# Two raw products side by side on smaller first loads, and later scales between partitions by DMA transposes

## The chip, the cores and the metric

The kernel runs on one core of a Trainium2 chip. The core has engines that each work through their own program in order: PE (TensorE, matrix products; PEld is its loading of the stationary operand), DVE (VectorE), ACT (ScalarE), POOL (GpSimd) and SP (SyncE), which here issues nearly all DMA transfers. Engines wait for each other through semaphores. The metric is the device time of one execution in microseconds (us); the median of several runs is compared. Differences under about 0.2% can't be told from run to run.

## What is computed

Two independent halves are joined along the last axis. A is attention with 32 heads of 32 and a sliding window of 256 over 2048 positions, between two projections; B is a Fourier mixing, two products with cosine and sine matrices on each side of x. All tensors are float32.

```python
def _A_ref(x, wqkv, wo):
    B, S, D = x.shape                # 1, 2048, 1024
    H = 32; Dh = D // H; W = 256
    qkv = (x @ wqkv).reshape(B, S, 3, H, Dh).transpose(2, 0, 3, 1, 4)
    q, k, v = qkv[0], qkv[1], qkv[2]
    scores = einsum("bhqd,bhkd->bhqk", q, k) * (Dh ** -0.5)
    scores = where(causal and within W, scores, -1e9)
    o = einsum("bhqk,bhkd->bhqd", softmax(scores), v)
    return o.transpose(0, 2, 1, 3).reshape(B, S, D) @ wo

def _B_ref(x, dft_seq_re, dft_seq_im, dft_hid_re, dft_hid_im):
    a = einsum("bsd,ed->bse", x, dft_hid_re)
    b = einsum("bsd,ed->bse", x, dft_hid_im)
    return einsum("ts,bse->bte", dft_seq_re, a) - einsum("ts,bse->bte", dft_seq_im, b)

return concatenate([A, B], axis=-1)
```

## The kernel before

**Split numbers and their scales.** A product of two float32 matrices is made from float16 parts: each operand is scaled by a power of two and split into a high and a low half (`split`, L124: ACT writes the high half, DVE the low one), and three products hi·hi, hi·lo, lo·hi are summed in PSUM. So every operand needs a scale before it can be split. `top` and `mean` (L142, L150) leave one number for each of the 128 partitions; `spread` (L157) reduces it to one column; and `scale_of` (L166) makes one number of the 128: PE transposes the column, broadcast over 128 columns, against the identity matrix `ident` into a PSUM tile `pt_...`, DVE reduces that to a maximum (`tensor_reduce`), cuts it to a power of two, and takes the reciprocal. In the head (`head[0]` true) the transposes sit in PE's order at a place written out by hand (L171); later (L174) they take a bank of the three that the products rotate through, and in the last stage the bank `pv` of the attention.

**Stages.** The head does the first four q products (`pq0_0` to `pq3_0`, four groups of weights `wq` against the first quarter of x) directly on the raw float32 data, eight matmuls each (`d_mm`, L736); the scale is applied only to their result (`d_out`, L890). A dozen-odd matmuls on zeros (`warm`) run first. A loop over `order` (L930) then makes all other q, k and v products in float16, 24 matmuls each, and from its step 22 on a generator, `attention`, weaves the attention's matmuls between them (`tick`, at a rate from a table). Small jobs are attached to steps by `at(n, ...)` (L398): a weight is loaded six steps before its first use, its `w_top` runs four before, `w_finish` (scale and split) three before. The last stage runs units of seven products each (`seven`), in which the jobs are attached to positions ("turns") by `do(n, turn, ...)`: for a unit's cosine or sine matrix `u`, `u_load` three units ahead, `u_top` two ahead at turns 0 and 2, `u_scale` at turn 6, and the splits `u_step` one unit ahead, at its turns 0 to 4.

**What sets the order.** A scheduler places instructions on each engine, with hand-set constraints: PE's matmuls follow one another as written (`mm`, L112, through `fixed`); DVE's in the head do too (`vec`, through `latest`). DMA issues on SP run in order, those of the attention behind one another (`line`): `t<-hl` transposes the softmax weights of a block (128x1024 float16), `raw_u` loads the next matrix. `behind` holds the latest DVE instruction of an attention block or product, and other DVE work is placed behind it.

**Memory.** `xin` (the split x) fills the tile `reg1`; `spare` is its tail. The pool `pa` holds the products' outgoing tiles, `yq`/`yk` and `yv`, two of each.

Of the kernel before, what the change touches and what calls it, by code (L numbers as in the profile page):

```python
# [12 lines left out]
BF16 = mybir.dt.bfloat16  # L13
U8 = mybir.dt.uint8
U32 = mybir.dt.uint32
AF = mybir.ActivationFunctionType
# [3 lines left out]
P = 128  # L20
S = 2048
D = 1024
H = 32
# [30 lines left out]
def fused_kernel(ctx: ExitStack, tc: tile.TileContext, xa, wqk, wv, wo, xb, wd, cs, out):  # L54
# [25 lines left out]

    ident = const.tile([P, P], F32, name="ident")
    make_identity(nc, ident)


# [11 lines left out]

    nbank, units_on = [0], []

# [35 lines left out]

    tops, head = {}, [True]


# [19 lines left out]
    def spread(key, n):  # L157
        t = tops.pop(key)
        if n > 1:
            t1 = small.tile([P, 1], F32, tag="top0", name=f"top1_{key}")  # L160
            vec(nc.vector.tensor_reduce, t1, t, axis=AX.X, op=ALU.max)
        else:
            t1 = t
        tops[key] = t1

    def scale_of(key, v, s, down=2.0 ** -14):  # L166

        if head[0]:
            pt = ps_s.tile([P, CH], F32, tag="s", name=f"pt_{key}")[:, :P]
            with tc.issue_after(fixed[0].ins) if fixed else nullcontext():  # L170
                fixed[:] = [nc.tensor.transpose(pt, tops.pop(key).to_broadcast([P, P]), ident)]  # L171
        else:
            pt = (ps_v.tile([P, CH], F32, tag="pv", name=f"pt_{key}") if units_on else bank(f"pt_{key}"))[:, :P]
            nc.tensor.transpose(pt, tops.pop(key).to_broadcast([P, P]), ident)  # L174
# [266 lines left out]
    def x_load(c, pool=None):  # L441
        for i in range(4):
            if c == 0 or c == 2 and i < 2:
                xraw[c, i] = praw(2 * c + i).rearrange("p (d t) -> p d t", t=CH)
                nc.sync.dma_start(xraw[c, i], xa[c, i])
# [105 lines left out]
    for (kd, g), n in use.items():  # L551
        if kd in "qk" and n >= 4:
            at(n - 6, w_load, kd, g)
            at(n - 4, w_top, kd, g)
            at(n - 3, w_finish, kd, g)
    for g in range(NG):
# [6 lines left out]
    at(7, strict.__setitem__, 0, False)  # L563
    at(7, head.__setitem__, 0, False)
    at(4, x_top, 2, (0, 1))
    at(5, x_top, 2, (2, 3))
# [7 lines left out]
    at(14, wv_top, 0)  # L574
    at(15, wv_scale, 0)
    for i, n in enumerate((15, 16, 16, 17)):
        at(n, wv_split, 0, (i,))
    at(15, wv_load, 1)
    at(18, wv_top, 1)
    at(19, wv_scale, 1)  # L580
    for i, n in enumerate((19, 20, 21, 21)):
        at(n, wv_split, 1, (i,))
# [136 lines left out]

    for i in range(WARM // 3):  # L720
        nc.tensor.matmul(wps, warm[:, :P], warm, start=True, stop=True)
    w_load("q", 0, first)
    x_load(0, first)
    for g in (1, 2, 3):
        w_load("q", g, first)
    x_load(1, first)
    x_load(2)
# [8 lines left out]
    def d_mm(g, ds):  # L736
# [3 lines left out]
        for d in ds:  # L740
            mm(direct[g], wraw["q", g][:, d], xraw[0, d // 2][:, d % 2], start=(d == 0), stop=(d == ND - 1))

# [136 lines left out]

    with tc.tile_pool(name="pa", bufs=2) as pa:  # L880
        def qk_out(kd, g, c, ps, f):
            y = pa.tile([P, 2, CH], F16, tag="yq", name=f"y{kd}{g}_{c}")
            behind_act[:] = [nc.scalar.activation(y[:, 0], ps, AF.Copy, scale=f)]
# [8 lines left out]

        w_top("q", 0)
        x_top(0, (0, 1, 2, 3))
        d_mm(0, range(0, 4))
        w_scale("q", 0)
        d_mm(0, range(4, 8))
        w_top("q", 1)
        d_mm(1, range(0, 1))
        x_scale(0)  # L900
        d_known(0)
        d_mm(1, range(1, 3))
        w_scale("q", 1)
        d_known(1)
        d_out(0)
        w_split("q", 0)
        w_top("q", 2)
        d_mm(1, range(3, 8))
        x_top(1, (0, 1))
        d_out(1)  # L910
        d_mm(2, range(0, 2))
        w_scale("q", 2)
        d_known(2)
        x_top(1, (2, 3))
        d_mm(2, range(2, 8))
        w_top("q", 3)
        d_mm(3, range(0, 2))
        x_scale(1)
        x_split(1, (0, 1))
        d_out(2)  # L920
        d_mm(3, range(2, 4))
        w_scale("q", 3)
        d_known(3)
        x_split(1, (2,))
        d_mm(3, range(4, 8))
        x_split(1, (3,))
        w_split("q", 1)
        d_out(3)

        for n, (kd, g, c) in enumerate(order):  # L930
# [154 lines left out]

    units_on.append(True)
# [159 lines left out]
```

## Time and profile before

| | |
|---|---|
| median of 3 runs | 1708.01 us (1707.69 to 1711.28) |
| profiled execution, its own time | 1705.92 us |
| its span (first to last instruction) | 1703.9 us |
| mean granted TensorE clock | 1.000 |
| share of the span busy: PE / DVE / ACT / POOL | 99% / 76% / 69% / 34% |
| mean busy share of the 16 DMA engines, 200 to 400 us | 1.02 |

A row of a timeline reads: start in us, length in us, engine, line, operation, what it writes <- what it reads, shapes, count, and in brackets how long the engine had been idle and what ended that. Rows of matmuls that follow one another are merged (x10); the length of a merged row goes to the end of its last matmul, which overlaps the next row's start. Names are the program's: `wx` is where the first quarter of x lands, `raw_wq` a raw weight, `reg` any of the large tiles `reg1` and `reg2`. A float32 matmul of 512 columns appears as two instructions, so eight `d_mm` steps are sixteen.

### The profile page before, as it was taken

How to read it: one execution, taken by the hardware profiler on the slowest of the kernel's cores; microseconds unless marked ns; L12 is line 12 of the kernel's file. 1: busy time of each engine (PE TensorE's matmuls, PEld its weight loads, DVE VectorE, ACT ScalarE, POOL GpSimd, SP SyncE). 2: the span in 40 equal slices, each digit the busy share in tenths (PEclk: the TensorE clock that was granted, in tenths of full speed). 3: DMA queues.
4: the chain of work that ended last, by engine and by line, in shares of the span. 5: the costliest groups of instructions: out<-in, count | busy, mean ns of one | idle time of the engine just before them, and what ended most of it. 6: DMA issues, size and time to landing. Idle time of an engine off the chain costs nothing.

```text
span 1703.9 us, 30860 instructions
## 1 busy us (share of the span) xinstructions
PE 1693.1 (99%) x10999; PEld 851.4 (50%) x10999; DVE 1301.6 (76%) x2225; ACT 1169.3 (69%) x2035; POOL 573.8 (34%) x874
## 2 busy tenths in 40 slices
PE   9999999999999999999999999999999999999999
PEld 4444555555555554555555555555555555444444
DVE  6847788887988688887678886688886698688442
ACT  4466666676877687888678886678877687563322
POOL 0000322334444341444423474433555425411000
PEclk9999999999999999999999999999999999999999
DMA  9747999999998995887998999986999976876431
GB/s 351 244 138 241 258 289 273 289 254 305 249 231 218 207 231 122 197 203 178 226 249 246 198 183 175 232 201 120 194 167 203 228 183 136 173 184 119 116 99 75
DMA packets 469898, 348.62 MB, mean 205 GB/s; under 512 B 376944, under 2 KB 409968, under 8 KB 468848
## 3 DMA queue, kind: packets, MB, share of 16 engines
q1 hardware_dynamic: 462064, 321.48, 75.3%
q0 software_dynamic: 7680, 25.17, 9.2%
q8 instruction: 86, 1.41, 0.4%
q14 instruction: 68, 0.56, 0.1%
HBM read 166.99 MB, written 106.17 MB: 160 GB/s over the span
## 4 chain that ended last, share of the span: by engine, by line
PE 80%; DVE 7%; ACT 4%; DMA 4%; issue 3%; POOL 2%; SPq 0%; DVEq 0%; POOLq 0%; ACTq 0%
PE p_a L114 22%; PE pv L114 13%; PE p_b L114 10%; PE pk L114 9%; PE pq L114 8%; PE p_c L114 5%; PE po_a L114 5%; PE s L114 3%; PE po_b L114 2%; PE far L114 1%; PE po_c L114 1%; DMA t<-hl 1%; DMA ots<-ot 1%; DVE reg L835 1%; DVE hl L270 1%
## 5 line engine op out<-in xcount | busy, mean ns | idle before, releaser
L266 ACT ACTIVATE s<-s,bias,escs 128x256 f32<-128x256 f32 (+1 forms) x512 | 270.0, 528 | 11.7
L284 POOL TENSOR_SCALAR_AFFINE_SELECT z<-t 128x512 f16<-128x512 f16 x224 | 187.0, 841 | 159.6 <-PE pv L114 142.3
L259 ACT ACTIVATE bias<-mx,pshift,escs 128x2 f32<-128x2 f32 x256 | 98.3, 384 | 171.6 <-DVE mx L256 171.3
L270 DVE TENSOR_TENSOR hl<-s,hl 128x512 f16<-128x512 f32 (+1 forms) x256 | 170.1, 665 | 56.0 <-ACT hl L269 55.2
L114 PEld LDWEIGHTS <-reg 128*128 128x128 f16 x1344 | 128.9, 97 | 141.7
L286 POOL TENSOR_SCALAR_AFFINE_SELECT t<-t 128x512 f16<-128x512 f16 x224 | 183.8, 829 | 11.4
L114 PE MATMUL p_a<-reg,un_c 128*128 128x512 f16 x768 | 181.2, 379 | 0.4 <-ACT p_c L1068 0.2
L263 POOL TENSOR_SCALAR mark<-bias 128x1 f32<-128x1 f32 x128 | 53.1, 415 | 363.0 <-ACT bias L259 356.5
L114 PE MATMUL pk<-reg,wu_k 128*128 128x512 f16 x768 | 174.4, 379 | 0.0
L256 DVE TENSOR_REDUCE mx<-s 128x2 f32<-128x512 f32 (+1 forms) x256 | 170.9, 668 | 3.4
L114 PE MATMUL pv<-reg,reg 128*128 128x512 f16 x768 | 172.7, 379 | 0.0
L114 PEld LDWEIGHTS <-un_c 128*128 128x128 f16 x1152 | 109.9, 97 | 121.3 <-issue 2.0
L114 PEld LDWEIGHTS <-un_b 128*128 128x128 f16 x1152 | 110.0, 97 | 117.8 <-issue 1.1
L114 PEld LDWEIGHTS <-un_a 128*128 128x128 f16 x1152 | 109.7, 97 | 116.3
L269 ACT ACTIVATE hl<-s 128x512 f16<-128x512 f32 (+1 forms) x256 | 148.8, 581 | 6.4 <-DMA t<-hl 1.0
L114 PE MATMUL pq<-reg,wu_q 128*128 128x512 f16 x672 | 151.3, 379 | 0.8 <-DVE reg L121 0.5
L114 PE MATMUL p_a<-reg,un_b 128*128 128x512 f16 x576 | 136.4, 379 | 0.4 <-DVE y L1036 0.3
L114 PE MATMUL p_b<-reg,un_b 128*128 128x512 f16 x576 | 136.4, 379 | 0.3 <-DVE reg L835 0.3
L114 PE MATMUL p_a<-reg,un_a 128*128 128x512 f16 x576 | 136.6, 379 | 0.0
L114 PE MATMUL p_c<-reg,un_a 128*128 128x512 f16 x576 | 136.5, 379 | 0.0
L254 DVE COPY_PREDICATED s<-upper,far 128x256 f32<-128x256 uint32 x224 | 94.3, 421 | 46.2 <-PE s L114 44.9
L114 PEld LDWEIGHTS <-qk 96*128 96x128 f16 x1056 | 87.9, 97 | 64.3 <-issue 1.8
(208 smaller groups left out, 3153.2 us busy)
## 6 DMA issues: line engine op xcount, KB each, us to landing
raw_u<-in_cs_dram SPq DMA_DIRECT2D x64, 512.0 KB, 4.9
qk<-qk SPq DMA_DIRECT2D x64, 384.0 KB, 4.9
out_dram<-y POOLq DMA_DIRECT2D x72, 256.0 KB, 6.1
raw_wd<-in_wd_dram SPq DMA_DIRECT2D x24, 512.0 KB, 5.2
vs<-yv SPq DMA_DIRECT2D x32, 264.0 KB, 4.4
vt<-vs SPq DMA_DIRECT2D x64, 132.0 KB, 4.5
raw_wo<-in_wo_dram SPq DMA_DIRECT2D x16, 512.0 KB, 8.1
qk<-yq SPq DMA_DIRECT2D x32, 256.0 KB, 3.4
```

The source lines that it names most:

```text
L114: fixed[:] = [nc.tensor.matmul(*args, **kwargs)]
L254: nc.vector.copy_predicated(s[:, :, P:], upper2, d["far"] if nb == 3 else never2)
L256: nc.vector.tensor_reduce(mx, sv, axis=AX.X, op=ALU.max, negate=True)
L259: nc.scalar.activation(bias, mx, AF.Identity, bias=pshift, scale=es)
L263: marks[:] = [nc.gpsimd.tensor_scalar(mark, bias[:, 0:1], 1.0, None, op0=ALU.mult)]
L266: nc.scalar.activation(sv[:, h], sv[:, h], AF.Exp, bias=bias[:, h:h + 1], scale=es)
L269: nc.scalar.activation(hi, sv, AF.Copy)
L270: behind[:] = [nc.vector.tensor_tensor(lo, sv, hi, op=ALU.subtract)]
L284: nc.gpsimd.affine_select(out=z, in_=pk, compare_op=ALU.is_gt, fill=0.0, base=0, pattern=[[0, 4], [-1, P]], channel_multiplier=1)
L286: nc.gpsimd.affine_select(out=pk, in_=pk, compare_op=ALU.is_ge, fill=0.0, base=0, pattern=[[0, 4], [1, P]], channel_multiplier=-1)
L835: nc.vector.tensor_tensor(lo, src, hi, op=ALU.subtract)
```

## The change

The diff has three parts: the head (nine smaller loads, the first two raw products interleaved, other jobs reordered), the scales after the head (from step 11 of the loop on, by DMA transposes on SP instead of PE), and buffers (one tag `y` with three tiles; `ident` placed in `spare`).

```diff
-    ident = const.tile([P, P], F32, name="ident")
+    ident = spare[:, :2 * P].bitcast(F32)
     make_identity(nc, ident)
...
     tops, head = {}, [True]
+    crossing, crossed = [None], {}
...
         tops[key] = t1
+        if crossing[0]:
+            pb = crossing[0].tile([P, P], F16, tag="pb", name=f"pb_{key}")
+            nc.vector.tensor_scalar(pb.bitcast(U16), t1.bitcast(U16)[:, 1:2].to_broadcast([P, P]), 0x7F80, None,
+                                    op0=ALU.bitwise_and)
+            pc = crossing[0].tile([P, 1, P], F16, tag="pc", name=f"pc_{key}")
+            with tc.issue_after(line[0].ins) if line else nullcontext():
+                nc.sync.dma_start_transpose(pc, pb)
+            crossed[key] = pc.rearrange("p a t -> p (a t)").bitcast(BF16)
 
     def scale_of(key, v, s, down=2.0 ** -14):
 
+        if key in crossed:
+            with tc.issue_after(behind[0].ins):
+                nc.vector.tensor_reduce(v, crossed.pop(key), axis=AX.X, op=ALU.max)
+            nc.vector.tensor_scalar(v, v, 2.0 ** -100, down, op0=ALU.max, op1=ALU.mult)
+            nc.vector.reciprocal(s, v)
+            return
...
-            at(n - 3, w_finish, kd, g)
+            at(n - 3 if n < 16 else n - 2, w_finish, kd, g)
...
+    at(11, lambda: crossing.__setitem__(0, pa))
...
-    at(15, wv_scale, 0)
-    for i, n in enumerate((15, 16, 16, 17)):
+    at(16, wv_scale, 0)
+    for i, n in enumerate((16, 17, 17, 18)):
...
-    for i in range(WARM // 3):
+    for i in range(WARM // 4):
         nc.tensor.matmul(wps, warm[:, :P], warm, start=True, stop=True)
-    w_load("q", 0, first)
-    x_load(0, first)
-    for g in (1, 2, 3):
+    for g in (0, 1):
+        wraw["q", g] = first.tile([P, ND, P], F32, tag="raw", name=f"raw_wq{g}")
...
+    def w_part(g, a, b):
+        nc.sync.dma_start(wraw["q", g][:, a:b], wqk[0, g][:, a:b])
+
+    def x_part(a, b):
+        nc.sync.dma_start(xraw[0, a // 2][:, a % 2:a % 2 + b - a], xa[0, a // 2][:, a % 2:a % 2 + b - a])
+
+    for f, args in ((w_part, (0, 0, 2)), (x_part, (0, 1)), (w_part, (1, 0, 2)), (x_part, (1, 2)), (w_part, (0, 2, 8)),
+                    (x_part, (2, 4)), (w_part, (1, 2, 8)), (x_part, (4, 6)), (x_part, (6, 8))):
+        f(*args)
...
-    with tc.tile_pool(name="pa", bufs=2) as pa:
+    with tc.tile_pool(name="pa", bufs=3) as pa:
         def qk_out(kd, g, c, ps, f):
-            y = pa.tile([P, 2, CH], F16, tag="yq", name=f"y{kd}{g}_{c}")
+            y = pa.tile([P, 2, CH], F16, tag="y", name=f"y{kd}{g}_{c}")
...
-        w_top("q", 0)
-        x_top(0, (0, 1, 2, 3))
-        d_mm(0, range(0, 4))
+        for g in range(3):
+            w_top("q", g)
+        x_top(0, (0, 1))
+        d_mm(0, (0,))
+        d_mm(1, (0,))
+        d_mm(0, (1,))
+        d_mm(1, (1,))
+        d_mm(0, (2, 3))
         w_scale("q", 0)
...
-                y = pa.tile([P, H // 2, VW], F16, tag="yv", name=f"yv{g}_{t}")
+                y = pa.tile([P, H // 2, VW], F16, tag="y", name=f"yv{g}_{t}")
...
     with tc.tile_pool(name="pb", bufs=1) as pb:
+        crossing[0] = pb
```

**PE in the head.** The names are `pq_0` for a raw product (its number tells which), `wx` for x, and `pt_` for a transpose of a scale. Before, PE's rows behind the warm-up were these:

```order
L114 MATMUL pq_0_171<-wx,raw_wq_132 128x512 x4
L171 MATMUL pt_wq_176<-ident,top_wq_162 128x128
L114 MATMUL pq_0_171<-wx,raw_wq_132 128x512 x4
L114 MATMUL pq_0_188<-wx,raw_wq_138 128x512
L171 MATMUL pt_x_190<-ident,top_x_169 128x128
L114 MATMUL pq_0_188<-wx,raw_wq_138 128x512 x2
L171 MATMUL pt_wq_200<-ident,top_wq_186 128x128
L114 MATMUL pq_0_188<-wx,raw_wq_138 128x512 x5
```

After the change the same engine has, from the end of the warm-up to the end of the first two products:

```order
L116 MATMUL pq_0_171<-wx,raw_wq_129 128x512
L116 MATMUL pq_0_173<-wx,raw_wq_130 128x512
L116 MATMUL pq_0_171<-wx,raw_wq_129 128x512
L116 MATMUL pq_0_173<-wx,raw_wq_130 128x512
L116 MATMUL pq_0_171<-wx,raw_wq_129 128x512 x2
L188 MATMUL pt_wq_179<-reg_83,top_wq_162 128x128
L116 MATMUL pq_0_173<-wx,raw_wq_130 128x512 x2
L188 MATMUL pt_wq_188<-reg_83,top_wq_164 128x128
L116 MATMUL pq_0_171<-wx,raw_wq_129 128x512 x2
L116 MATMUL pq_0_173<-wx,raw_wq_130 128x512 x2
L188 MATMUL pt_x_201<-reg_83,top_x_195 128x128
L116 MATMUL pq_0_171<-wx,raw_wq_129 128x512 x2
```

The two products take turns, so that PE uses each piece of x twice before it needs the next, and the transpose of x's scale has moved from the ninth matmul to behind the twelfth. The number of raw matmuls and of the head's transposes is the same; two matmuls of the warm-up are gone.

**A scale in the last stage, on PE.** Before, around the scale of the unit's matrix that DVE reads at about 920 us (`pt_u` the transpose, `p_16` the unit's product):

```order
L114 LDWEIGHTS reg_83
L114 MATMUL p_16_b<-reg_83 128x512
L174 MATMUL pt_u_11514<-ident,top_u_11391 128x128
L114 LDWEIGHTS un_b
L114 MATMUL p_16_a<-reg_83,un_b 128x512
```

After, the row of `pt_u` is gone here and at 56 other places; no other row of PE's order behind the head has moved.

**The same scale on SP and DVE, after.** SP's rows there are these (`pb` is the column written out over 128 columns, `pc` its transpose, `t<-hl` that of a block's softmax weights):

```order
L784 DMA raw_u_0_11518<-in_cs_dram 128x1024
L289 DMA_TRANSPOSE t_11420<-hl_11417 128x8x128
L174 DMA_TRANSPOSE pc_u_11430<-pb_u_11428 128x1x128
L352 DMA_TRANSPOSE ot_1_0_11488<-ohl_1_0_11485 128x4x128
```

And DVE's, from the `hl` whose transpose SP issues just ahead of it to the reduction that needs `pc` (`pb_u_11428` stands six rows above the first of these):

```order
L287 TENSOR_TENSOR hl_11417<-s_11403,hl_11417 128x512
L123 SCALAR_TENSOR_TENSOR un_b<-raw_u_0_11120,sc_u_11343,un_b 128x1024
L1072 SCALAR_TENSOR_TENSOR y_6790<-p_16_b,fu_11182,y_6790 128x512
L271 COPY_PREDICATED s_11524<-upper,far 128x2x128
L273 TENSOR_REDUCE mx_11530<-s_11524 128x2
L271 COPY_PREDICATED s_11588<-upper,far 128x2x128
L287 TENSOR_TENSOR hl_11538<-s_11524,hl_11538 128x512
L181 TENSOR_REDUCE sc_u_11552<-pc_u_11430 128x1
```

The reduction stands in DVE's row with everything of the attention behind it, and it now needs a transfer that can be issued only behind that block's own transpose.

More of the change, by code (lines that the diff above doesn't have):

```diff
@@ L14 @@
 U8 = mybir.dt.uint8
+U16 = mybir.dt.uint16
 U32 = mybir.dt.uint32
@@ L95, in fused_kernel @@
     nc.gpsimd.memset(pshift, PSHIFT)
-    nbank, units_on = [0], []
+    nbank = [0]
     def bank(name):
@@ L172, in scale_of @@
         else:
-            pt = (ps_v.tile([P, CH], F32, tag="pv", name=f"pt_{key}") if units_on else bank(f"pt_{key}"))[:, :P]
+            pt = bank(f"pt_{key}")[:, :P]
             nc.tensor.transpose(pt, tops.pop(key).to_broadcast([P, P]), ident)
@@ L442, in x_load @@
         for i in range(4):
-            if c == 0 or c == 2 and i < 2:
-                xraw[c, i] = praw(2 * c + i).rearrange("p (d t) -> p d t", t=CH)
+            if c == 2 and i < 2:
+                xraw[c, i] = praw(4 + i).rearrange("p (d t) -> p d t", t=CH)
                 nc.sync.dma_start(xraw[c, i], xa[c, i])
@@ L579, in fused_kernel @@
     at(18, wv_top, 1)
-    at(19, wv_scale, 1)
-    for i, n in enumerate((19, 20, 21, 21)):
+    at(20, wv_scale, 1)
+    for i, n in enumerate((20, 21, 21, 22)):
         at(n, wv_split, 1, (i,))
@@ L718, in warm_up @@
             nc.tensor.matmul(wps, warm[:, :P], warm, start=True, stop=True)
-    for i in range(WARM // 3):
+    for i in range(WARM // 4):
         nc.tensor.matmul(wps, warm[:, :P], warm, start=True, stop=True)
-    w_load("q", 0, first)
-    x_load(0, first)
-    for g in (1, 2, 3):
+    for g in (0, 1):
+        wraw["q", g] = first.tile([P, ND, P], F32, tag="raw", name=f"raw_wq{g}")
+    for i in range(4):
+        xraw[0, i] = praw(i).rearrange("p (d t) -> p d t", t=CH)
+    def w_part(g, a, b):
[5 more added lines that the diff above has]
+        f(*args)
+    for g in (2, 3):
         w_load("q", g, first)
+    raw0 = [wraw["q", g] for g in range(4)]
     x_load(1, first)
@@ L740, in d_mm @@
         for d in ds:
-            mm(direct[g], wraw["q", g][:, d], xraw[0, d // 2][:, d % 2], start=(d == 0), stop=(d == ND - 1))
+            mm(direct[g], raw0[g][:, d], xraw[0, d // 2][:, d % 2], start=(d == 0), stop=(d == ND - 1))
     units = []
@@ L891, in d_out @@
             qk_out("q", g, 0, direct.pop(g), f0[:, g:g + 1])
-        w_top("q", 0)
-        x_top(0, (0, 1, 2, 3))
-        d_mm(0, range(0, 4))
-        w_scale("q", 0)
-        d_mm(0, range(4, 8))
-        w_top("q", 1)
-        d_mm(1, range(0, 1))
+        for g in range(3):
[6 more added lines that the diff above has]
+        d_mm(0, (2, 3))
+        w_scale("q", 0)
+        d_mm(1, (2, 3))
+        x_top(0, (2,))
+        w_scale("q", 1)
+        x_top(0, (3,))
+        d_mm(0, (4, 5))
+        d_mm(1, (4, 5))
         x_scale(0)
         d_known(0)
-        d_mm(1, range(1, 3))
-        w_scale("q", 1)
         d_known(1)
+        w_split("q", 0)
+        x_top(1, (0,))
+        d_mm(0, (6, 7))
+        d_mm(1, (6, 7))
         d_out(0)
[L906 to L909, printed above, removed]
         d_out(1)
-        d_mm(2, range(0, 2))
+        d_mm(2, (0,))
         w_scale("q", 2)
         d_known(2)
-        x_top(1, (2, 3))
-        d_mm(2, range(2, 8))
+        x_top(1, (1, 2, 3))
+        d_mm(2, range(1, 8))
         w_top("q", 3)
-        d_mm(3, range(0, 2))
+        d_mm(3, (0,))
         x_scale(1)
-        x_split(1, (0, 1))
         d_out(2)
-        d_mm(3, range(2, 4))
+        x_split(1, (0, 1), behind_act)
+        d_mm(3, (1, 2, 3))
         w_scale("q", 3)
         d_known(3)
-        x_split(1, (2,))
+        x_split(1, (2, 3), behind_act)
         d_mm(3, range(4, 8))
-        x_split(1, (3,))
         w_split("q", 1)
@@ L1083, in seven @@
             hook(pos)
-    units_on.append(True)
     perm, turns = [(nbank[0] + 1 + k) % 3 for k in range(3)], [0]
     with tc.tile_pool(name="pb", bufs=1) as pb:
+        crossing[0] = pb
         ybufs = [pb.tile([P, 2, CH], F32, name=f"y{k}") for k in range(3)]
```

## The prediction

> **What bounds the kernel now.** First the shares of the engines and the chain that ended last:
>
> ```profile
> PE 1693.1 (99%) x10999; PEld 851.4 (50%) x10999; DVE 1301.6 (76%) x2225; ACT 1169.3 (69%) x2035; POOL 573.8 (34%) x874
> PE 80%; DVE 7%; ACT 4%; DMA 4%; issue 3%; POOL 2%; SPq 0%; DVEq 0%; POOLq 0%; ACTq 0%
> ```
>
> PE is busy for 1693.1 of 1703.9 us, and no other engine is above 76%. A busy PE need not be at its peak, so I look next at whether its matmuls follow one another at a constant step; a long undisturbed row of them is:
>
> ```profile
> 51.34 20.88 PE L114 MATMUL pq<-reg,wu_q 128*128 128x512 f16 x96 [0.33 <-DVE yq L121]
> 72.05 0.27 PE L174 MATMUL pt_x<-ident,top_x 128*128 128x128 f32 x1
> 72.16 2.10 PE L114 MATMUL pq<-reg,wu_q 128*128 128x512 f16 x9
> ```
>
> 96 matmuls start within 72.05 - 51.34 = 20.71 us, a step of 0.216 us each, with no room between. The third view is what PE waited for:
>
> ```profile
> PE wps L721 <- DVE reg L713: 1.2, 1, 1.2
> PE far L114 <- DVE s L254: 1.2, 1, 1.2
> PE s L114 <- DMA qk<-qk: 1.0, 1, 1.0
> PE pq L114 <- DMA wx<-in_xa_dram: 0.9, 1, 0.9
> ...
> PE pq L114 <- DVE reg L121: 0.5, 1, 0.5
> PE pq L114 <- DVE yq L121: 0.3, 1, 0.3
> PE pt_x L174 <- DVE top_x L121: 0.3, 1, 0.3
> ```
>
> All of it is a few us, a third of it (wx, reg, yq, pt_x) in the head, 2.2 us (far and s) in the attention. So PE's own list of instructions sets the time: what is taken off that list is gained, what delays another engine costs only when it reaches PE.
>
> **The change, part by part.** *The transposes behind the head.* Those on PE's list now:
>
> ```profile
> L174 PE MATMUL pt_u<-ident,top_u x32: 272/272/275, 630.9 to 1515.8; 128*128 128x128 f32 x32
> L174 PE MATMUL pt_wk<-ident,top_wk x8: 273/273/275, 81.4 to 523.3; 128*128 128x128 f32 x8
> L174 PE MATMUL pt_xp<-ident,top_xp x8: 272/273/275, 124.3 to 324.8; 128*128 128x128 f32 x8
> L174 PE MATMUL pt_wq<-ident,top_wq x4: 273/274/303, 354.3 to 499.8; 128*128 128x128 f32 x4
> ...
> L174 PE MATMUL pt_wv<-ident,top_wv x2: 273/273/273, 97.1 to 117.9; 128*128 128x128 f32 x2
> L174 PE MATMUL pt_wd<-ident,top_wd x2: 273/273/273, 336.3 to 391.3; 128*128 128x128 f32 x2
> L174 PE MATMUL pt_wo<-ident,top_wo x1: 303/303/303, 249.1 to 249.1; 128*128 128x128 f32 x1
> ```
>
> These 32 + 8 + 8 + 4 + 2 + 2 + 1 = 57 go; only two of x stay. Each record is 0.27 us long, but that is its passage through a pipeline: in the rows above, the matmul behind `pt_x` starts 72.16 - 72.05 = 0.11 us after it. The price of one lies between 0.11 and 0.27 us, so between 6.3 and 15.5 us for 57. I take 0.11, the step, since the starts before and after it show no other delay: **-6.3 us**.
>
> *The start.* These rows carry it:
>
> ```profile
> 1.25 3.67 PE L721 MATMUL wps<-reg 128*128 128x512 f16 x10 [1.25 <-DVE reg L713]
> 4.11 0.32 PEld L721 LDWEIGHTS <-reg 128*128 128x128 f16 x2 [0.18 <-issue]
> 4.40 1.06 ACT L155 ACTIVATE junk<-raw_wq 128x1024 uint8<-128x1024 f32 x1 [2.32 <-DMA raw_wq<-in_wqk_dram]
> 5.68 1.22 DVE L121 TENSOR_REDUCE top_x<-wx 128x1 f32<-128x1024 f32 x1 [4.50 <-DMA wx<-in_xa_dram]
> 5.80 3.67 PE L114 MATMUL pq<-wx,raw_wq 128*128 128x512 f32 x8 [0.88 <-DMA wx<-in_xa_dram]
> 11.37 1.06 ACT L155 ACTIVATE junk<-raw_wq 128x1024 uint8<-128x1024 f32 x1 [5.82 <-DMA raw_wq<-in_wqk_dram]
> ```
>
> The first load of 0.5 MB has landed at 4.40, the second (x) at 5.68, and the first product waits for both. The sixth has landed at 11.37: (11.37 - 4.40) / 2.5 MB = 2.8 us per MB. Now the first matmul needs 128 + 256 KB, 0.375 MB, so about 4.40 - 0.125 x 2.8 = 4.1 us. The warm-up loses the last two of ten matmuls; the eighth starts at about 4.11 (the load of weights for it, and the step there is already the short one), and is over at 4.33. I take 4.4 for the first product, between the ends 4.33 (loads no obstacle) and 5.80 (as now): **-1.4 us**. The later pieces by the same 2.8 us per MB: 1.625 MB (x's second half MB) at 7.5, the rest of the second weight at 8.6, x's third at 10.0, its last at 11.4. The raw matmuls run from 5.80 to 34.01 (the row is below): four products of eight, two instructions each, and six transposes, (28.2 - 0.7) / 64 = 0.43 an instruction, 0.86 a matmul. With two products in turn these pieces are wanted at 4.4 + 4 x 0.86 = 7.8, 9.6, 11.5 and 15.0. All are there, the first by 0.3 us only.
>
> *Behind the raw products.* Now PE stops three times:
>
> ```profile
> 34.01 2.97 PE L114 MATMUL pq<-reg,wu_q 128*128 128x512 f16 x13
> 37.47 12.89 PE L114 MATMUL pq<-reg,wu_q 128*128 128x512 f16 x59 [0.49 <-DVE reg L121]
> 50.69 0.32 PE L174 MATMUL pt_x<-ident,top_x 128*128 128x128 f32 x1 [0.32 <-DVE top_x L121]
> ```
>
> By steps, 13 x 0.216 = 2.8 us, so it could have gone on at 36.8 and did at 37.47: 0.65 lost. 59 steps end at 50.2 instead of 50.69, 0.5 lost; and from 50.69 + 0.11 to 51.34 another 0.5: together 1.7 us. The cause is DVE, which gets to the split of the second quarter of x late:
>
> ```profile
> 29.85 4.27 ACT L127 ACTIVATE reg<-raw_x,vx 128x1024 f16<-128x1024 f32 x4 [5.34 <-DVE vx L121]
> 34.72 0.75 DVE L121 SCALAR_TENSOR_TENSOR yq<-pq,f,yq 128x512 f16<-128x512 f32 x1 [1.21 <-ACT yq L883]
> ```
>
> In the new order its transpose stands behind one matmul of the fourth raw product instead of two, and the raw product's exit (`yq`) goes ahead of the four splits, not between them. The transpose comes at 4.4 + 25 x 0.86 + 4 x 0.11 = 26.3 (now 28.64, by the same rows' steps), the scale a us later, `yq` is out at 28.2, ACT's four splits end near 31.8 (4.27 us for four), and DVE's halves at 29.9, 31.1, 33.2 and 34.5 (1.24 each, a scale between). The raw products end at 34.01 - 1.4 = 32.6; pieces three and four are wanted at 32.6 + 12 x 0.216 = 35.2 and 36.5. So all three stops go, with DVE 4 us ahead of where it is now and PE 3: **-1.7 us**, with ends 0 (they move along) and -1.7. Against it stands the transpose of the first quarter's scale: DVE reduces the last piece (landed 11.4, but behind another scale, so 12.6 to 13.9) and needs 0.3 more, and PE comes to it at 14.9; if it slips, PE stands for tenths: +0.1.
>
> *What is added elsewhere.* For each scale DVE writes a tile of 128x128 and drops one of its small steps; reductions go on over 128 columns. SP issues 57 more transposes, each an eighth of `t<-hl` in size. None is on PE. What matters is the wait: DVE's reduction now holds up everything behind it until the transfer has landed. The rows at the place that the order lists show:
>
> ```profile
> 917.55 0.64 DVE L270 TENSOR_TENSOR hl<-s,hl 128x512 f16<-128x512 f32 x1
> 919.99 0.27 DVE L121 TENSOR_REDUCE sc_u<-pt_u 128x1 f32<-128x128 f32 x1
> 923.99 1.57 DVE L121 SCALAR_TENSOR_TENSOR un_a<-raw_u,sc_u,un_a 128x1024 f16<-128x1024 f32 x1 [2.30 <-ACT un_a L127]
> 918.33 1.23 SPq L272 DMA_TRANSPOSE t<-hl  x1
> DMA to landing us min/median/max: 2.3/4.7/12.3
> ```
>
> `hl` ends at 918.2, SP is on its transpose from 918.33 to 919.56, and can then issue the new one. A transpose lands 2.3 us after issue at the least and 4.7 in the median, so at 921.9 to 924.3; DVE comes to the reduction at about 921 (some two us later than now, three more rows stand ahead of it). It stands for 1 to 3 us there, in place of the 2.30 us that it idles a little later anyway, and the split that follows is for a matmul one unit (some 20 us) on. At most other places more DVE rows lie between. I put **+0.5 us** on PE for all of it; the ends are 0 and the rival below.
>
> Sum: -6.3 - 1.4 - 1.7 + 0.1 + 0.5 = **-8.8 us**, which from the profiled 1705.92 us (1703.9 of span and 2.0 around it) makes 1697.1. The median of the runs is 2.1 us higher than that execution, 1708.01, and so I forecast **1699.2 us**.
>
> *A rule against this change.* The page "VectorE: DVE Perf Modes" of the Trainium skill, "The three transpose paths" and "Rules for kernel authors", gives 390 ns for a 128x128 transpose on TensorE and 1309 ns by DMA, and says to take TensorE where a result in PSUM will do, as it does here. By its prices, as an estimate, 57 x (1.309 - 0.390) = +52 us if each stood on the path. The rows above disagree on what is to be compared: PE gives up 0.11 us, and a transfer's 2.3 us and more cost nothing while other DVE work covers them. Where they are not covered the rule would be right, and that is the first rival.
>
> **The rivals.** *DVE waits for the transposes (slower).* How much DVE can stand for is read from the windows; the second pair counts the transposes there:
>
> ```profile
> 200.00:400.00 200.00, 200.00 (x1361) 102.32 (x1360) 166.55 (x305) 136.27 (x242) 66.71 (x133) 1.00 1.02 277
> 600.00:800.00 200.00, 199.93 (x1435) 103.91 (x1434) 173.49 (x316) 165.95 (x304) 79.93 (x115) 1.00 0.78 183
> ...
> 200.00:400.00 200.00, 3.34 (x12) 1.00 1.02 277
> 600.00:800.00 200.00, 2.18 (x8) 1.00 0.78 183
> ```
>
> DVE has 33.5 us to spare for 12 transposes in the first and 26.5 for 8 in the second. Uncovered, at the median of 4.7 us, it would lack 56.4 - 33.5 = 23 and 37.6 - 26.5 = 11 us, and PE's scores would wait for it: 1699.2 + 34 = 1733. It decides from a mean stand of about 3.5 us, where the first window lacks 8.5 us and the gain is eaten up. For it: DMA is full there (1.02), and a transpose can take 12.3 us. Against it: the changed order leaves DVE more rows between at most of the 57 than the seven of the place above. Chance 0.09.
>
> *The transposes' room fills again (no change).* If the attention's pace in the middle is set by the full DMA engines, PE stands for the 6.3 us that it no longer works; only the head's 3 us remain: 1705.0. Against it: PE waited for DMA just 1.0 us behind the head. Chance 0.10.
>
> *The head does not do what it says.* The small loads land no earlier (packets of 1 KB instead of 4), and the stops move along: 1699.2 + 3.1 = 1702.3, still faster by more than 0.2% (3.4 us). Chance 0.13.
>
> **How the numbers follow.** The forecast has 0.68, with a range of its own from 1695 (the attention's waits of 2.2 us go too, and half of the unsure pieces come out better) to 1702. The range over 8 in 10 goes from 1694.5 to 1705.5, which takes in the weak head and the refilled room; outside lie most of the slow rival and a price of a transpose above 0.2 us. Faster: 0.68 + 0.13 = 0.81; same 0.10; slower 0.09.
>
> **What would show it.** In the changed profile, the first `pq` should start near 4.4 us and the first row with `wu_q` near 32.6, with no gap behind it. PE should have 57 + 2 instructions less and its steps of 0.216 us unbroken. DVE's waits should have a row `sc_u` <- DMA `pc_u<-pb_u` of some tens of us at most, and PE's waits for `s` and `far` should stay at a few us. I am wrong if PE has new waits for DVE of more than 5 us, if the first product still starts at 5.8, or if the sum of PE's busy time falls by less than 5 us.

## The result, and the profile after the change

The kernel became **slower**: a median of 1728.42 us (1726.21 to 1730.97) against 1707.85 us (1707.21 to 1711.28) for the kernel before, a ratio of 1.0118 (95% interval 1.0105 to 1.0131). The forecast was 1699.2, with a range up to 1705.5. The profiled execution has a span of 1724.2 us and a mean clock of 0.996. Ratios throughout are of fast executions alone; three far slower ones (2284.64 us with the later reduction, 4606.31 and 10215.32 us of the kernel before) are left out of them.

First the shares and the chain that ended last, after the change:

```profile
PE 1694.2 (98%) x10940; PEld 846.1 (49%) x10940; DVE 1305.5 (76%) x2225; ACT 1170.4 (68%) x2035; POOL 571.8 (33%) x874
PE 69%; DVE 12%; DMA 7%; ACT 6%; issue 5%; POOL 1%; SPq 0%; DVEq 0%; ACTq 0%; POOLq 0%
```

PE has 59 instructions fewer (57 transposes, two warm-up matmuls), yet its busy time did not fall, and PE holds 69% of the chain instead of 80%: DVE went from 7 to 12, DMA from 4 to 7. If every PE instruction is given the median step of its shape (a step is the time to the start of the next one), the list sums to 1687.0 us before and 1679.3 after, 7.7 us less, as the steps promised; but the steps that were over 0.02 us longer than their median took 36.6 us beyond it, against 10.0 before. Some 24 of the 36.6 are idle time of PE. So the question is what PE waited for. The view of its waits (total us, times, longest), after:

```profile
PE p_a L116 <- ACT p_c L1104: 5.7, 2, 3.2
PE p_a L116 <- DVE y L1072: 4.8, 4, 2.5
PE far L116 <- DVE s L271: 3.9, 3, 2.2
PE s L116 <- DMA qk<-qk: 2.2, 1, 2.2
PE p_b L116 <- DVE reg L866: 1.7, 1, 1.7
PE pq L116 <- DMA wx<-in_xa_dram: 1.6, 1, 1.6
```

Before, the largest row was 1.2 us. None of these rows names a transfer of a scale (`pc_...`); those are one step further back, in DVE's waits:

```profile
DVE sc_u L181 <- DMA pc_u<-pb_u: 15.5, 6, 4.2
DVE vxp L181 <- DMA pc_xp<-pb_xp: 2.4, 2, 2.0
DVE scw L181 <- DMA pc_wk<-pb_wk: 2.3, 1, 2.3
DVE vwd L181 <- DMA pc_wd<-pb_wd: 1.6, 1, 1.6
```

DVE stood 21.8 us in ten stops. One of them, followed through the timelines of DVE, SP and PE (start, length, engine, line; what had been waited for in brackets):

```profile
942.85 0.24 DVE L170 TENSOR_SCALAR pb_u<-top_u 128x128 uint16<-128x128 uint16 x1
945.62 3.19 SPq L784 DMA_DIRECT2D raw_u<-in_cs_dram  x2
949.38 1.24 SPq L289 DMA_TRANSPOSE t<-hl  x1
950.67 1.24 SPq L174 DMA_TRANSPOSE pc_u<-pb_u  x1
956.74 0.29 DVE L181 TENSOR_REDUCE sc_u<-pc_u 128x1 f32<-128x128 bf16 x1 [3.55 <-DMA pc_u<-pb_u]
970.39 0.74 DVE L1072 SCALAR_TENSOR_TENSOR y<-p_a,fu,y 128x512 f32<-128x512 f32 x1
...
965.92 2.75 PE L116 MATMUL p_b<-reg 128*128 128x512 f16 x12
971.18 3.33 PE L116 MATMUL p_a<-reg,un_b 128*128 128x512 f16 x8 [2.51 <-DVE y L1072]
974.67 1.03 PE L116 MATMUL p_a<-reg,un_b 128*128 128x512 f16 x4
```

The tile `pb_u` is ready at 943.1. SP comes to it only at 950.67, behind loads and an attention transpose; it lands at 956.7, and DVE has stood for 3.55 us. From there to 971 DVE has one gap, of 0.76 us, and does not catch up: `y`, which empties the bank `p_a`, ends at 971.1, and PE, which needs that bank, has stood 2.51 us. DVE's spare time exists as a mean, not at that place. Over all 57 transfers the trace gives 3.6 us from the ready tile to SP's issue in the mean (8.9 at most) and 3.7 from issue to landing.

The stop has a second price. The eight matmuls behind it take 3.33 us, up to 0.43 each; a row of eight at 0.22 each takes 1.89 (at 977.07 in the same trace). The windows show why (busy times and counts of PE, PEld, DVE, ACT, POOL, then PE's granted clock, the DMA engines' busy share and their GB/s):

```profile
968.00:971.20 3.20, 0.69 (x5) 0.22 (x3) 3.17 (x7) 2.18 (x4) 1.80 (x2) 0.92 0.20 22
971.20:975.00 3.80, 3.80 (x14) 1.58 (x14) 3.22 (x6) 1.56 (x4) 1.60 (x4) 0.62 1.03 234
975.00:980.00 5.00, 5.00 (x49) 2.73 (x47) 2.67 (x6) 4.58 (x9) 3.23 (x5) 1.00 1.04 172
```

The clock is down behind the stop and then comes back: about 1.4 us more, and since slow matmuls count as busy, PE's busy time hides it. The same follows these three stops (a mean clock of 0.66, 0.54 and 0.56 in the 3.5 to 3.7 us behind them), and not the stop of 2.2 us for `qk` at 419.1 (1.00):

```profile
348.41 0.22 PE L116 MATMUL far<-qk 96*128 96x128 f16 x1 [2.25 <-DVE s L271]
1482.94 4.30 PE L116 MATMUL p_a<-reg,un_c 128*128 128x512 f16 x12 [3.17 <-ACT p_c L1104]
1524.07 4.22 PE L116 MATMUL p_a<-reg,un_c 128*128 128x512 f16 x12 [2.49 <-ACT p_c L1104]
```

Last the head, PE's timeline after:

```profile
1.25 3.59 PE L739 MATMUL wps<-reg 128*128 128x512 f16 x8 [1.25 <-DVE reg L731]
4.63 3.65 PE L116 MATMUL pq<-wx,raw_wq 128*128 128x512 f32 x8
9.92 1.96 PE L116 MATMUL pq<-wx,raw_wq 128*128 128x512 f32 x4 [1.64 <-DMA wx<-in_xa_dram]
34.70 5.56 PE L116 MATMUL pq<-reg,wu_q 128*128 128x512 f16 x25
```

The first product starts at 4.63, but the next piece of x holds PE for 1.64 us before 9.92, and the float16 rows begin at 34.70 instead of 34.01, now without the three stops behind them.

### The profile page after: what moved, and what is told of

Its sections match the earlier page's. It is cut to its first block, busy times and chain, and to the rows that moved or that the text cites. A ratio compares the mean times of both kernels' runs of the same rounds, so it can differ in the third digit from the quotient of the medians.

```text
span 1724.2 us, 30812 instructions
## 1 busy us (share of the span) xinstructions
PE 1694.2 (98%) x10940; PEld 846.1 (49%) x10940; DVE 1305.5 (76%) x2225; ACT 1170.4 (68%) x2035; POOL 571.8 (33%) x874
## 4 chain that ended last, share of the span: by engine, by line
PE 69%; DVE 12%; DMA 7%; ACT 6%; issue 5%; POOL 1%; SPq 0%; DVEq 0%; ACTq 0%; POOLq 0%
PE p_a L116 18%; PE pv L116 10%; PE pq L116 9%; PE p_b L116 8%; PE pk L116 7%; PE po_a L116 5%; PE p_c L116 4%; PE po_b L116 2%; PE s L116 2%; DVE raw_u L823 2%; DMA t<-hl 2%; DVE hl L287 1%; DMA pc_u<-pb_u 1%; ACT s L283 1%; DVE reg L866 1%
## 5 line engine op out<-in xcount | busy, mean ns | idle before, releaser
L301 POOL TENSOR_SCALAR_AFFINE_SELECT z<-t 128x512 f16<-128x512 f16 x224 | 181.4, 816 | 161.6 <-PE pv L116 142.5
```

Of the source, the lines that this page charges most:

```text
L301: nc.gpsimd.affine_select(out=z, in_=pk, compare_op=ALU.is_gt, fill=0.0, base=0, pattern=[[0, 4], [-1, P]], channel_multiplier=1)
```

## The experiments

Each run was compared with the kernel before on the same chip; ratios are to that, since chips and executions differ by a few us (before itself ran from 1705.1 to 1713.7 in the first set). One thousandth is 1.7 us. With up to 32 executions a side the intervals are narrow enough to tell some differences under 0.2%.

**Which part loses.** Four kernels: all 57 transposes back on PE; the head as before; the units' 32 back on PE; the stream's 25 back on PE. The edits, on the changed kernel:

```diff
-    at(11, lambda: crossing.__setitem__(0, pa))      # out: stream's 25 on PE (first, fourth run)
-        crossing[0] = pb                             # out: units' 32 on PE (first, third run)
+        crossing[0] = None
+    ident = const.tile(...)                          # a place of its own, outside spare (first, third, fourth run)
# second run: x_load, loads, warm-up, d_mm order of the kernel before
```

> The changed kernel with all 57 transposes behind the head put back on PE: the new head alone. Theory (the loss of 20.6 us against before lies in DVE's waits for the transfers, not in the head): as before less what the head gains, about 1 us by the first f16 row (34.70 against 34.01) and the three stops of 1.7 us that are gone, so 1705.5 to 1708, no row with pc among DVE's waits, PE's step never at 0.43 us behind the head. Rival (the new head's later loads delay the stream behind it, and the clock falls there too): 1712 or more.

> The changed kernel with the head as before: the 57 DMA transposes alone. Theory: the whole loss is here, 1727 to 1731, with DVE waiting about 20 us for pc in some ten stops and PE stopping over 2 us at three or four places. Rival (head and transposes each cost something): 1715 to 1722.

> The changed kernel with the 32 transposes of the units (the scales u) put back on PE, the 25 before them by DMA. Theory: three of the four places where the clock fell (971, 1483, 1524) and most of DVE's 15.5 us for pc_u are in the units, so about two thirds of the 20.6 us go: 1710 to 1717. Rival (the loss is spread by the DMA queues, wherever the transposes are): loss in proportion to the count, 25 of 57, so 1717 or more.

> The changed kernel with the 25 transposes of the stream put back on PE, the 32 of the units by DMA: the other half of the same question. Theory: the losses of 300 to 450 us go (about 8 us, less 25 x 0.11 = 2.8 us that PE works again): 1720 to 1724. If the two halves add up, this one's and the last one's gains together make the 20.6 us to within 3 us; rival (a stop early shifts all that comes later, so that the halves don't add): they miss it by more than 5.

Measured: head alone 1.0009 (0.9996 to 1.0023); transfers alone 1.0158 (1.0127 to 1.0189); units on PE 1.0041 (1.0022 to 1.0059); stream on PE 1.0112 (1.0080 to 1.0144). So the loss is the transfers', and most of it the units'. The head alone does not gain. Whether the two groups add stays open: against the changed kernel's 20.2 us, moving the units back gives 13 (some 4 us of doubt) and the stream 1 (some 6).

**What of a transfer costs.** The list alone (each partition uses its own maximum, nothing is sent); the transfers sent but unread; plain copies sent, unread; transposes of a fixed tile, unread.

```diff
-            crossed[key] = pc.rearrange("p a t -> p (a t)").bitcast(BF16)
+            crossed[key] = pb.bitcast(BF16)                        # all four
-                nc.sync.dma_start_transpose(pc, pb)                # list alone: no pc at all
+                nc.sync.dma_start(pc.rearrange("p a t -> p (a t)"), pb)               # copies
+                nc.sync.dma_start_transpose(pc, upper.bitcast(F16)[:, :P])            # fixed tile
```

> The changed kernel without its 57 transfers: each partition takes its own maximum as scale, and the maximum over the partitions is left out; DVE's instructions stay the same (its reduction reads its own tile). This is what the shorter list of PE is worth alone. Theory (the waits cost 27 us, the list gives back about 7): 1699 to 1703, PE's stops as before or fewer. Rival (PE's list is not what bounds; before is paced by transfers that vary from run to run): 1706 to 1710, within 0.2% of before.

> As the last, but the 57 transfers are issued and nobody reads them. Theory (DVE's waiting for them is the whole loss): within 3 us of the last run. Rival (SP, whose issue of one takes 1.2 us, and the queue behind it delay the attention's own transposes and loads): at least a third of the 27 us lost, 1710 or more, with stops for s, far and qk.

> As the run with unread transfers, but each of the 57 is a plain copy of the same 32 KB instead of a transpose, from the same tile and at nearly the same place of SP's queue; nobody reads them, each partition takes its own maximum. The unread transposes cost 11.6 us over the kernel without them (1.0048 against 0.998 of before). Theory (a transpose holds SP for some 1.2 us each and the queue behind it for longer): a copy costs little, 0.997 to 1.001 of before (1704 to 1711). Rival (what costs is that SP, in order, waits for DVE's tile, whatever is sent): as with the transposes, 1.003 to 1.007.

> As the run with unread transfers, but the 57 transposes read a tile that never changes, so that SP waits for nothing of DVE's; nobody reads them, each partition takes its own maximum. If the transposes themselves cost (theory): 1.003 to 1.007 of before, as there. If SP's wait for DVE's tile is the cost (rival): 0.997 to 1.001.

| kernel | ratio to before | interval |
|---|---|---|
| nothing sent | 0.9980 | 0.9969 to 0.9992 |
| copies, unread | 1.0009 | 0.9999 to 1.0020 |
| transposes of a fixed tile, unread | 1.0032 | 1.0019 to 1.0044 |
| transposes of the scales, unread | 1.0048 | 1.0032 to 1.0064 |
| the changed kernel: the same, read by DVE | 1.0118 | 1.0105 to 1.0131 |

PE's order is the same in all five, DVE's in the first four; in the changed kernel DVE's differs at 116 of 2225 places, so the last step holds this shift too. Nothing sent gained 3.4 us of before, half of the 7 that I expected. My theory of that moment, that DVE's wait is the whole loss, fell: of the 23.6 us between the first row and the last, 11.6 are there when nobody reads the transfers, and 12.0 come with the reading (each good to some 3 us). Inside the 11.6, a plain copy takes about 5, a transpose in its place some 4 more; what SP's wait for the tile adds (the step to the fourth row) is within the doubt. In the two middle runs the scheduler put the issues at other places of SP's queue, and they ran on another chip, so the steps to them and from them are rough. The attention's own transposes land a little later (the view of DMA issues, median us to landing), and PE's waits for DVE grow, while its longest one, for `qk`, does not. By what path the sending reaches PE is not shown further than this. Nothing sent:

```profile
t<-hl SPq DMA_TRANSPOSE x256, 4.7
...
PE s L116 <- DMA qk<-qk: 4.6, 1, 4.6
PE p_a L116 <- DVE y L1069: 2.8, 4, 1.4
```

The transposes of the scales sent, unread:

```profile
t<-hl SPq DMA_TRANSPOSE x256, 4.9
...
PE p_a L116 <- DVE y L1072: 6.1, 5, 2.5
PE s L116 <- DMA qk<-qk: 3.2, 1, 3.2
PE far L116 <- DVE s L271: 1.9, 3, 0.8
```

**Two ways round the wait.** Issue by ACT, and a later reduction:

```diff
-                nc.sync.dma_start_transpose(pc, pb)
+            nc.scalar.dma_start_transpose(pc, pb)
```

```diff
-                do(n - 2, 6, u_scale, n)
-                for step, turn in enumerate((0, 1, 1, 2, 3, 4)):
+                do(n - 1, 0, u_scale, n)
+                for step, turn in enumerate((1, 2, 2, 3, 4, 5)):
```

> The changed kernel with the 57 transfers issued by ACT instead of SP. In the trace of the changed kernel the tile to be sent lies ready for up to 8.9 us (4.0 in the mean) until SP comes to its issue, since SP first waits for the attention's hl, and landing takes another 3.7. Theory (what makes DVE wait is SP's order, not the transfer): issue within 1 us of the tile, landing 2 to 4 us later, DVE waits for pc under 5 us, 1703 to 1712. Rival (the transfer itself lands late behind the other traffic, or ACT now stands as DVE did): 1720 or more.

> The changed kernel with the units' reduction and its six splits one product later (some 5 us), the 25 of the stream as they are. Theory: the units' waits for pc_u go from 15.5 us to under 5 and with them the stops behind 620 us, so the 20.2 us lost shrink to the stream's part, 7 us by the run with the units on PE, less 32 x 0.11 = 3.5 us: 1711 to 1715. Rival (the splits are late for the product then, PE waits for un_a, un_b or un_c): 1722 or more with such rows among PE's waits.

Measured 1.0576 (1.0545 to 1.0608) and 1.0234 (1.0198 to 1.0270): both far worse. With ACT, DVE's wait for `pc` fell to 1.2 us in one stop, as expected, but these rows are new, the first in SP's waits, the second in PE's:

```profile
SPq L288 <- DMA pc_u<-pb_u: 107.9, 20, 12.2
...
PE far L116 <- DVE s L270: 45.1, 19, 10.8
```

SP's transposes of the attention waited for ACT's to land. ACT's queue stood the other way round, 96.9 us in 35 stops until one of SP's had landed. In that trace no transfer of a scale is ever in flight together with one of the 320 attention transposes; in the changed kernel's, where all go through SP, 60 pairs are. The page "DMA: Bandwidth & Descriptors" of the Trainium skill, section "Silent corruption: two transposing streams in flight at once", says that transposes issued from SP and from ACT must not be in flight together, and that the later ones have to wait until the earlier are complete; the trace agrees that they do wait, SP 107.9 us and ACT 96.9. So this run does not tell whether SP's order or the transfer makes DVE wait.

The later reduction has one long stand and late operands (DVE's waits, then PE's):

```profile
DVE sc_u L181 <- DMA pc_u<-pb_u: 18.1, 3, 12.2
...
PE p_a L116 <- DVE y L1072: 9.3, 8, 2.8
PE p_b L116 <- DVE un_b L123: 5.0, 5, 2.1
```

The rival held: PE now waits for `un_b`, so the splits had no 5 us to give away. And DVE's longest wait grew from 4.2 to 12.2 us: there `pc_u` is issued right behind eight 0.5 MB loads of `wo` and lands 15.1 us after its issue.

**Transposes on PE in bf16, and the head.** If a transpose on PE costs 0.109 us, one of half the width costs 0.056, with nothing to wait for. Of the maximum only the exponent is kept, so the upper 16 bits will do:

```diff
-    ident = const.tile([P, P], F32, name="ident")
+    ident = const.tile([P, P], BF16, name="ident")
-            nc.tensor.transpose(pt, tops.pop(key).to_broadcast([P, P]), ident)
+            nc.tensor.matmul(pt, tops.pop(key).bitcast(BF16)[:, 1:2].to_broadcast([P, P]), ident, start=True, stop=True)
```

> The kernel before, with every transpose left on PE but fed with the upper half of the maximum's bits as bf16 (the exponent is all that the scale keeps, so the result is the same) and a bf16 identity. A 128x128 f32 step is 0.109 us, an f16 one 0.056: 65 x 0.053 = 3.4 us off PE's list with no new wait. Theory: 0.997 to 0.999 of before. Rival (what goes off the list comes back as stops): 1.000.

> The kernel before with the new head alone: the smaller loads, the warm-up of 8 and the order of the raw products; the scales' places and the buffers of the outputs as before. The run with the head alone so far had those two changed as well and gave 1.0009 (0.9996 to 1.0023). Theory (the head gains about 1 us and nothing else moves): 0.998 to 1.000. Rival (the head's shift by a microsecond changes which of the attention's transfers are late, and eats the gain): 1.000 to 1.002 with larger stops for qk or far.

> The new head (with the buffers and the scales' places of the changed kernel) and all 65 transposes on PE in bf16: the two changes that add no wait for a transfer, together. By sums: the head alone gave 1.0009 and bf16 alone 0.997 of before, so 0.998 if they add; theory (the head's 1.0 us at the end of the raw products is real, its loss later is made up of stops that another order need not have): 0.996 to 0.999. Rival (the later stops belong to the new head): 1.000 or more, with PE stopping over 2 us at the qk load near 412 us and at the scores near 1245 us.

> As the last, with the head's loads in another order: the second quarter of both weights and of x (0.125 and 0.25 MB each) ahead of the rest of the weights. In the new head the piece that I put at 7.5 us landed at 9.8 and PE stopped 1.6 us for it. Theory (it landed late since 0.5 MB and more of the weights' rest was ahead of it and the queued loads share the engines): the stop at 9.8 goes below 0.5 us and the first f16 row comes 1 us or more earlier than in the last run. Rival (the stop moves to the next pieces, since the loads as a whole come no faster): a stop of over 1 us before the fifth or the seventh pair of matmuls, first f16 row within 0.5 us of the last run.

> Kernel before with bf16 transposes on PE, the new head and the outputs' three shared buffers, but every scale at its place of before (the runs of head and bf16 together had the splits of some weights one product later, and there PE stopped 1.7 us at 243 us for wu_k in both). Behind the head the order of all engines is that of the run of bf16 alone, which runs beside it. Theory (the head's 1.0 us is real; what took it back was the later split): the stops at 36.2 us and 243 us are gone and the ratio is 0.0006 below that of the run beside it, 0.996 to 0.998. Rival (any head that comes earlier loses it again, since the stops for qk near 413 us and for the scores near 1245 us are set by transfers): equal to the run beside it or above, with those stops longer by about a microsecond.

> The kernel before with its transposes on PE in bf16, nothing else changed, beside the last run on one chip. Theory: 0.997 of before again (0.9958 to 0.9981 there), 3.4 us by the list and the rest by where the stops fall. Rival (that run was lucky in its stops): 0.998 to 1.000.

| kernel | ratio to before | interval |
|---|---|---|
| bf16 on PE | 0.9970 | 0.9958 to 0.9981 |
| the same again | 0.9977 | 0.9966 to 0.9987 |
| new head alone, two `yq` buffers as before | 1.0018 | 1.0007 to 1.0029 |
| new head, three buffers, later scales, bf16 | 0.9991 | 0.9981 to 1.0002 |
| the same, other order of the first loads | 0.9988 | 0.9976 to 0.9999 |
| new head, three buffers, scales where they were, bf16 | 0.9967 | 0.9954 to 0.9979 |

The kernel with bf16 transposes was faster than the kernel before, and so than the changed one, both times. The head needs the third buffer: with two, the third output waits for the store of an earlier one, and the float16 rows start late (PE in the run with the new head alone):

```profile
36.22 0.38 PE L114 MATMUL pq<-reg,wu_q 128*128 128x512 f16 x1 [2.03 <-ACT reg L127]
37.54 6.81 PE L114 MATMUL pq<-reg,wu_q 128*128 128x512 f16 x23 [0.95 <-DVE reg L121]
```

The same run also has longer stops for `far` (3.4 us) and `qk` (1.8) than before, as its rival had said. With three buffers, PE is 0.7 to 1.5 us ahead of before at 56 us, in every run that has them and the new head. The runs with later scales on PE lose that again by 250 us. At 243 us three transposes now stand behind one another, and the next product waits for a bank until DVE has read them (PE in the run with head and bf16):

```profile
243.73 2.53 PE L116 MATMUL pk<-reg,wu_k 128*128 128x512 f16 x11 [1.55 <-DVE scw L123]
```

With the scales where they were, the stop is gone, and the last row is 0.0010 below the bf16 run beside it on the same chip. That is what a head gain of 1 us would give, but the intervals overlap. The other order of the loads removed the stop at 9.9 us and got another in its place, PE now waiting for ACT's pass over the weight:

```profile
11.61 0.23 PE L188 MATMUL pt_wq<-ident,top_wq 128*128 128x128 bf16 x1 [1.41 <-ACT junk L158]
```

The float16 rows began at 34.60 instead of 34.80: its rival held, the loads as a whole come no faster.

**What a stop costs.** Rows of 60 matmuls, each waiting for a chain of DVE instructions of growing length; nothing of the reference is computed.

```diff
+    for turn in range(2):
+        for k in (1, 2, 3, 4, 5, 6, 7, 8):
+            ...                       # k DVE instructions on the last row's result
+            ps = row(z, 60)           # 60 matmuls 128x512 f16 that read DVE's tile
```

> A kernel of its own that computes nothing of the reference: rows of 60 matmuls of 128x512 in f16, each row waiting for a chain of DVE instructions on the row before, of a length that grows over eight stops, all twice. It prices a stop of PE. In the changed kernel, stops of 2.25 us and more were followed by some 8 matmuls at 0.427 us instead of 0.216, stops of 1.6 us were not. Theory (a threshold between 1.7 and 2.3 us): rows behind shorter stops keep 0.216 us from their first matmul, rows behind longer ones begin with 3 to 3.5 us at 0.427 and so lose 1.6 us more. Rival (the slow matmuls there come from something else that the same delay brings): all rows keep 0.216 up to at least 4 us.

Its PE timeline at six of the sixteen stops (in brackets):

```profile
32.73 13.12 PE L41 MATMUL ps<-z,w 128*128 128x512 f16 x60 [1.74 <-DVE z L52]
48.02 13.12 PE L41 MATMUL ps<-z,w 128*128 128x512 f16 x60 [2.17 <-DVE z L52]
63.75 14.81 PE L41 MATMUL ps<-z,w 128*128 128x512 f16 x60 [2.60 <-DVE z L52]
81.58 14.44 PE L41 MATMUL ps<-z,w 128*128 128x512 f16 x60 [3.02 <-DVE z L52]
99.47 13.12 PE L41 MATMUL ps<-z,w 128*128 128x512 f16 x60 [3.45 <-DVE z L52]
...
136.53 15.96 PE L41 MATMUL ps<-z,w 128*128 128x512 f16 x60 [4.31 <-DVE z L52]
```

A row takes 13.12 us behind stops of up to 2.17, both times. From 2.60 on it takes 1.3 to 2.8 us more, in nine rows of ten (the exception is the 3.45 above). So the theory held in this: the slow matmuls of the changed kernel are the stop's own price. But the length of a stop does not decide alone. In the clock records of the traces, half clock comes in pieces of 3.413 us, one, two or three in a row, and within a trace they start whole multiples of 3.413 us apart, wherever the stops lie. These are such pieces of time, two around the stop of 2.60 and two around the exception (busy times of PE, PEld, DVE and POOL, then the clock, the DMA engines' busy share and GB/s):

```profile
60.39:63.80 3.41, 0.81 (x5) 0.20 (x4) 2.37 (x6) 0.00 (x0) 1.00 0.00 0
63.80:67.21 3.41, 3.41 (x9) 1.22 (x10) 0.00 (x0) 0.00 (x0) 0.50 0.00 0
94.53:97.94 3.41, 1.49 (x7) 0.49 (x5) 1.78 (x5) 0.00 (x0) 1.00 0.00 0
97.94:101.35 3.41, 1.88 (x9) 0.90 (x10) 1.37 (x4) 0.00 (x0) 1.00 0.00 0
```

The stop of 2.60 us lies whole in one piece, and the next one has half clock; the stop of 3.45 is divided, 1.92 and 1.53 us, and nothing follows. The other traces bear this out. Of the pieces at full clock in all nineteen, each of the 43 in which PE was idle for 2.04 us or more was followed by half clock, none of the 8953 with less than 1.88 us was, and of the twelve between 5 were. So a short stop can cost as much as a long one: this one, in the run with the other order of loads, shares its piece with 0.33 us of idle time ahead of it and is followed by 3.41 us at half clock, while a stop of 3.57 us at 1257.1 in the run with the units on PE is divided and costs nothing more.

```profile
243.43 4.87 PE L116 MATMUL pk<-reg,wu_k 128*128 128x512 f16 x14 [1.55 <-DVE scw L123]
```

## Why the prediction was wrong

**The list (-6.3 us): right.** By median steps PE's list is 6.2 us shorter with the 57 transposes gone (1685.5 in the run with the head alone, 1679.3 with nothing sent). As time, the ratios of these two kernels differ by 0.0029, 4.9 us, with some 3 of doubt.

**"What is added elsewhere ... +0.5 us for all of it": the step that failed.** It should have been about +24 us: 11.6 for sending and 12.0 for reading what was sent. Three things went wrong in it.
- I let SP issue the new transpose as soon as it was through with the attention's. In the trace a ready tile lies 3.6 us in the mean before SP reaches it, so from tile to landing it is 7.4 us, not 2.3 to 4.7. At the place that I worked out, I put the stand at 1 to 3 us. There it was none: DVE came to that reduction at 934.8 us, when `pc_u` had landed. Stands of 0.4 to 4.2 us came at ten other places, and what they do to PE I had put at half a microsecond.
- I called SP's 57 extra issues free because none is on PE. Sent and unread they cost more than the whole forecast gain.
- I measured DVE's room by its idle sum over 200 us windows, and set the slow rival's threshold at a mean stand of 3.5 us. The mean stand was 21.8/57 = 0.4 us. The rival's time (1733) came near, but by luck for the most part: DVE's idle time did not run out as a sum (it is busy for 76% after as before); single stands of 2 to 4 us fell on rows with no room behind them, and half of the loss came with nobody reading a transfer.

The sign to watch for was set too wide for that reason: I allowed DVE "some tens of us" of waits for `pc_u`, and 15.5 us were enough. The other signs did their work: new waits of PE for DVE of more than 5 us in all, and a busy time that did not fall.

**The start (-1.4) and the three stops (-1.7, +0.1): right in mechanism, one size wrong.** The first product came at 4.63 for 4.4, and the stops behind the raw products went. But the piece put at 7.5 us held PE until 9.92: the rate of 2.8 us per MB, read from loads of 0.5 MB in their old order, did not hold for the new ones. In the trace the fourth load is in at 5.40 and the fifth, 0.375 MB of a weight, only at 8.50, and the first 3.0 MB are in at 13.33, where 3.0 MB were in at 11.28 before. So the weak-head rival was partly true: the first pieces land earlier, the later ones do not. That stop took 1.64 us back, so 1.0 us remained of 3.0; and the head kernel with two buffers loses even that, a condition that I had not named.

**The rule on transposes.** The page "VectorE: DVE Perf Modes" of the Trainium skill, "Rules for kernel authors", would have the transpose on TensorE where PSUM will do. The runs bear it out here, by a different account than two durations: 11.6 us lost with nobody reading the transfers, and 12.0 more with the reading.

**Where the time went**, by the start of the same matmul in the four profiles (warm-up and transposes not counted; us, and the difference to before):

| matmul | before | nothing sent | sent, unread | changed kernel |
|---|---|---|---|---|
| 160th | 56.3 | -1.5 | -1.1 | -1.0 |
| 2000th | 364.0 | -3.4 | -2.3 | +2.2 |
| 2600th | 450.2 | +2.4 | +6.0 | +6.1 |
| 7000th | 1061.1 | +3.4 | +7.0 | +12.0 |
| 10000th | 1502.2 | +2.2 | +8.3 | +16.4 |
| last | 1699.7 | +2.1 | +12.6 | +20.0 |

These are single executions on different chips, each good to some us: nothing sent ends 2.1 us later here, though its ratio to before on the same chip is 0.9980. The changed kernel is still ahead at 276 us (-2.3 at the 1400th matmul), behind by the 2000th, and it loses the rest in a few places, not everywhere. Some of the list's gain also goes where nothing is sent: near 413 us PE waits for the `qk` load in nearly every kernel, 1.0 us before and 4.6 there, and behind the 4.6 two pieces of half clock (6.83 us from 411.6 on) cost it some 2 us more. So a list that arrives earlier waits longer for the same load. The "room fills again" rival was partly true.

## What to carry to other kernels

A wait that is taken off the bounding engine and put on another one in order is paid where that engine has no room behind it; read the room at the place, from tile to landing and past every queue in between, not as an idle sum. Before moving a small operation off the bounding engine, make it cheaper where it is: half the width gained 0.2 to 0.3%, where moving it lost 1.2% with the new head and 1.6% without. Sending with nobody reading can be run apart from sending and reading, and should be before either is called free.

## What the hardware showed beyond that

- In these traces PE's clock changes only at points 3.413 us apart. It fell to half (0.427 instead of 0.216 us a matmul) behind every piece between two such points with 2.04 us or more of idle time of PE, and behind none with less than 1.88, so a stop from 1.55 us on can drop it, and one of 3.57 us need not. The page "TensorE: Matmul & The Clock Gate" of the Trainium skill, "HAM oscillation — how this bites in real kernels", names idle gaps of over 3.4 us as those to avoid; the rows at 2.60 us differ, and the measurement decides.
- A 32 KB transpose that nobody reads cost some 0.2 us of the program each (11.6 / 57, the 11.6 good to some 3), though no engine but SP had a new instruction for it.
- Transposes issued by two engines were kept from being in flight together, at 107.9 us of SP's waiting for `pc_u` and 96.9 us of ACT's queue for SP's.
